# Attention outputs two units behind, and shared value rows written in by GpSimd

## The chip, the cores and the metric

The program runs on one core of a Trainium2 chip. The metric is device time in microseconds (us) of one execution; the median of three runs of the kernel before is 739.56 us (738.72 to 741.37).

## The reference, cut to what matters

Attention over 8 batches and 8 heads, with 512 local tokens and 32 global tokens of width 64, feeds a mixture of eight experts:

```python
k_all = concatenate([k_g, k_l]); v_all = concatenate([v_g, v_l])
out_g = softmax(scale * q_g @ k_all.T) @ v_all              # a global token sees everything
s_ll = where(abs(i - j) <= 32, scale * q_l @ k_l.T, -1e9)   # a local token sees a band
out_l = softmax(concatenate([scale * q_l @ k_g.T, s_ll])) @ v_all   # ... and the 32 global rows
x = concatenate([out_g, out_l]).reshape(4608, 512)
# each token goes to one of 8 experts (capacity 576, greedy by gate value): relu(x @ w1[e]) @ w2[e]
```

All inputs are float32. The host only rearranges them.

## The kernel before

**Two stages.** The attention takes the first 260 us of the profiled execution; the routing of tokens and the experts take the rest. The change touches the attention alone.

**Units.** For each batch there are ten units: eight `Local` units (half of the 512 rows of one pair of heads) and two `Glob` units (the global rows of four heads). 80 units in all. A unit passes through six steps, each an engine's work:

- `a`: scores on PE (TensorE) into the PSUM tile `S` (L143 of a local unit, L210 of a global one);
- `e`: mask and maximum on DVE (VectorE), which writes `p` and `nm` (L149, L151; L216 to L218);
- `f`: the exponentials on ACT (ScalarE) (L157; L228 to L234);
- `c`: transposes of `p` on PE into PSUM tile `T` (L162, L242), then a copy out of PSUM to `pt` or `pgt` on ACT (L269) or DVE (L271), three of five on ACT;
- `d`: the outputs on PE, `pt` times the value tile `vw`, into PSUM tile `O` (L174, L252), and their scaling by the row sum on DVE (`ls`, `xs`: L177, L178, L182). A global unit also stores its result to DRAM from SP (SyncE), four DMAs (L261).

**The order.** Each engine works through its own list in program order. The main loop, over `i`, puts into the lists: loads, `a` and `e` of unit i+2, `d` of unit i-1, `c` of unit i, `f` of unit i+2, and then the extra work of that step (the store of a finished batch `xd<-xs`, L186, and transposes and products for the gate, L277 to L292). So PE runs, in each step, the scores of a unit two ahead, the outputs of the unit one behind, and the transposes of the present one.

**The loads.** SP loads, for each of 32 pairs of heads, the queries `q` (272 KB), the keys `qk` (432 KB) and the value tile `vw` (1040 KB). It does so in step with the work: before each load a tiny DMA (`pace<-nm`, L123) waits for the maximum of the latest unit. GpSimd (POOL) spreads each `q` over a zero-padded tile `qz` in two copies (L87). Value tiles have six buffers.

**The value tile.** A local unit's 32 rows see a window of 128 key rows: three blocks of 32 local rows and the block of 32 global rows. `vw` holds, for each of 16 windows and two heads, these 128 rows on 128 partitions, 65 wide (64 values and a one, whose product is the row sum). So each tile holds the same 32 global rows 16 times for each head, all loaded from DRAM. In windows with odd number they lie on partitions 64 to 95, in those with even number on 32 to 63.

Of the kernel before, what the change touches and what calls it, by code (L numbers as in the profile page):

```python
# [8 lines left out]
F32 = mybir.dt.float32  # L9
# [9 lines left out]
B, H, SL, SG, D = 8, 8, 512, 32, 64  # L19
# [6 lines left out]
NB = SL // 128  # L26
NW = SL // 32
NZ = 6
NP = H // 2
# [6 lines left out]
def ap_of(t, offset, dims):  # L36
    return bass.AP(tensor=t.tensor, offset=t.offset + offset, ap=dims)
# [28 lines left out]
def attention(ctx, tc, A, consts, xd, pace, ident, L, nbatch, rt=None):  # L66
    nc = tc.nc
    ac = ctx.enter_context(tc.tile_pool(name="ac", bufs=1))
    ld = ctx.enter_context(tc.tile_pool(name="ld", bufs=3))
    wk = ctx.enter_context(tc.tile_pool(name="wk", bufs=3))  # L70
    ps = ctx.enter_context(tc.tile_pool(name="ps", bufs=2, space=PSUM))

    G = [(b, g) for b in range(nbatch) for g in range(2)]
    qk, vw, xs = {}, {}, {}

    def load_qk(b, p):
        t = ld.tile([128, KW], F32, name="qk", bufs=5)
# [10 lines left out]
        return spread  # L88

    def load_v(b, p):  # L90
        t = ld.tile([128, 2, NW, D + 1], F32, name="vw", bufs=6)
        nc.sync.dma_start(t.rearrange("p h w d -> p (h w d)"), A["vw"][b, p])
        vw[b, p] = t

    qz = [ac.tile([128, QW // 32, 2, 32], F32, name=f"qz{i}") for i in range(NZ)]
# [1 line left out]
    mask = ac.tile([128, 2 * NB, 128], F32, name="mask")  # L97
    wg = ac.tile([128, 4, 32], F32, name="wg")
# [27 lines left out]
    class Local:  # L126
# [32 lines left out]
        def c(s):  # L159
            t = ps.tile([128, NB, 128], F32, name="T", bufs=3)  # L160
            for c in range(NB):
                nc.tensor.transpose(t[:, c, :], s.p[:, c, :], ident)  # L162
            s.pt = wk.tile([128, NB, 128], F32, name="pt", bufs=3)
            evac(s.pt, t, bool(s.u) if s.b == nbatch - 1 and s.q == NP - 1 else None)

        def d(s):
            b, q, u = s.b, s.q, s.u
            o = ps.tile([128, 2, 2, D + 1], F32, name="O", bufs=2)
            for h in range(2):
                for k in range(2):  # L170
                    for r in range(4):
                        jj = 4 * k + r
                        lo = 64 * (jj % 2) + 32 * h
                        nc.tensor.matmul(o[32 * r:32 * r + 32, k, h, :], s.pt[:, jj // 2, lo:lo + 32],  # L174
                                         vw[b, q][:, h, 8 * u + jj, :], start=True, stop=True)
            ls = wk.tile([128, 2, 2], F32, name="ls", bufs=4)
            nc.vector.tensor_scalar(ls, o[:, :, :, D], 1e-9, None, op0=ALU.add)  # L177
            nc.vector.reciprocal(ls, ls)  # L178
            if q + u == 0:
                xs[b] = wk.tile([128, NB, DM], F32, name="xs", bufs=2)  # L180
            dst = xs[b][:, 2 * u:2 * u + 2, 128 * q:128 * q + 128].rearrange("p k (h d) -> p k h d", h=2)
            nc.vector.tensor_tensor(dst, o[:, :, :, 0:D], ls[:, :, :, None].to_broadcast([128, 2, 2, D]),  # L182
                                    op=ALU.mult)

    def store(b):
        nc.sync.dma_start(ap_of(xd, (b * S + SG) * DM, [[DM, 128], [128 * DM, NB], [1, DM]]), xs[b])  # L186

    class Glob:
# [22 lines left out]

        def e(s):
            b, g = s.b, s.g
            m = wk.tile([128, 8], F32, name="gm", bufs=2)
            s.m = m
            nc.vector.tensor_reduce(m[:, 0:1], s.sa, axis=AX.X, op=ALU.max)  # L216
            nc.vector.tensor_reduce(m[:, 1:2], s.sb, axis=AX.X, op=ALU.max)
            nc.vector.tensor_scalar(m[:, 2:3], m[:, 0:1], m[:, 1:2], -SCALE, op0=ALU.max, op1=ALU.mult)  # L218
# [16 lines left out]
                                 bias=m[:, 2:3], scale=SCALE, accum_out=m[:, 5:6])  # L235

        def c(s):
            s.pt = wk.tile([128, 6, 128], F32, name="pgt", bufs=2)
            for lo, n in ((0, 4), (4, 2)):
                t = ps.tile([128, NB, 128], F32, name="T", bufs=3)  # L240
                for k in range(n):
                    nc.tensor.transpose(t[:, k, :], s.p[:, lo + k, :], ident)  # L242
                evac(s.pt[:, lo:lo + n], t[:, :n])

        def d(s):
            b, g = s.b, s.g
            m = s.m
            o = ps.tile([128, D], F32, name="O", bufs=2)
            for k in range(6):
                for r in range(4):  # L250
                    h = 4 * g + r
                    nc.tensor.matmul(o[32 * r:32 * r + 32, :], s.pt[:, k, 32 * r:32 * r + 32],  # L252
                                     vw[b, h // 2][:, h % 2, 3 * k + 1 if k < 5 else 14, 0:D],
                                     start=(k == 0), stop=(k == 5))
            nc.vector.tensor_reduce(m[:, 6:7], m[:, 3:6], axis=AX.X, op=ALU.add)
            nc.vector.tensor_scalar(m[:, 6:7], m[:, 6:7], 1e-9, None, op0=ALU.add)
            nc.vector.reciprocal(m[:, 6:7], m[:, 6:7])
            xg = wk.tile([128, D], F32, name="xg", bufs=2)
            nc.vector.tensor_scalar(xg, o, m[:, 6:7], None, op0=ALU.mult)
            for r in range(4):  # L260
                nc.sync.dma_start(ap_of(xd, b * S * DM + (4 * g + r) * D, [[DM, SG], [1, D]]),  # L261
                                  xg[32 * r:32 * r + 32, :])
# [3 lines left out]
    def evac(dst, src, act=None):  # L266
        nev[0] += 1
        if nev[0] % 5 < 3 if act is None else act:
            nc.scalar.activation(dst, src, AF.Copy)  # L269
        else:  # L270
            nc.vector.tensor_copy(dst, src)  # L271
# [92 lines left out]
    units = []  # L364
# [8 lines left out]
    extra, wide = {}, {}  # L373
    GS = (0, 2, 4, 6, 8, 9)
    for b in range(nbatch):
        last = b == nbatch - 1
        s0 = 10 * (b + 1) + 1
        gl = gate_units(b, lambda b=b: gsrc[b // 4], 32 + b // 4, 1) if b % 4 == 3 else []
        lo = last_gate(b) if last else gate_units(b, lambda b=b: xs[b], 4 * b, NB)
        extra.setdefault(s0 + (-1 if last else 1), []).append(lambda b=b: store(b))  # L380
        if last:
            extra.setdefault(s0 - 5, []).append(lambda b=b: load_gx(b // 4))
            for k in range(3):
                extra.setdefault(s0 - (6, 4, 1)[k], []).append(lo[k])
        else:
            for k, f in enumerate(lo):
                (wide if k == 4 else extra).setdefault(s0 + (k if b == nbatch - 2 else GS[k]), []).append(f)
            if gl:
                extra.setdefault(s0 + 2, []).append(lambda b=b: load_gx(b // 4))
                for k, f in enumerate(gl):  # L390
                    (wide if k == 4 else extra).setdefault(s0 + 10 + k, []).append(f)
# [7 lines left out]
    nu = len(units)  # L399
    first = rt.setup(slice(0, 24), True) if rt else None  # L400
    LA = 2
    for i in range(-LA, nu + 3):
        if rt and i == 2:
            rt.load()
        if rt and i == 12:
            rt.prepare()
        if i + LA < nu:
            if i >= 0 and nl[1] < nl[0]:
                behind()
                load_v(*P[nl[1]])  # L410
                nl[1] += 1
            elif nl[0] < len(P) and nl[0] <= pairidx(units[i + LA]) + 3:
                if i >= 0:
                    behind()
                load_qk(*P[nl[0]])(nc.gpsimd)
                nl[0] += 1
            units[i + LA].a()
            units[i + LA].e()
            if i + LA == 0:
                spread1(nc.vector)  # L420
        if 1 <= i <= nu:
            units[i - 1].d()
        rest = [f() for f in wide.get(i, [])]
        if 0 <= i < nu:
            units[i].c()
        if i + LA < nu:
            units[i + LA].f()
        for f in rest + extra.get(i, []):
            f()
        if rt and i >= nu - 9:  # L430
            next(first, None)
# [733 lines left out]
def _layout(q_l, k_l, v_l, q_g, k_g, v_g, moe_w_gate, moe_w1, moe_w2):  # L1165
# [3 lines left out]
    qk = np.concatenate([qT, kT], axis=3).reshape(B, NP, 2 * D, QW + KW)  # L1169
# [1 line left out]
    st = [32 * ((3 * j + 1) // 2) for j in range(NW)]  # L1171
    vs = np.concatenate([vs, np.ones_like(vs[..., :1])], axis=3)
    vw = np.stack([vs[:, :, t:t + 128] for t in st], axis=3)
    vw = vw.reshape(B, NP, 2, 128, NW, D + 1).transpose(0, 1, 3, 2, 4, 5).reshape(B, NP, 128, 2 * NW * (D + 1))
    w1 = moe_w1.reshape(E, 4, 128, 2, FF // 2).transpose(3, 0, 2, 1, 4).reshape(2 * E * 128, 2 * FF)
    w2 = moe_w2.reshape(E, 2, 4, 128, DM).transpose(1, 0, 3, 2, 4).reshape(2 * E * 128, 4 * DM)
    wg = np.zeros((128, 4, 32), f)
    wg[:, :, :E] = moe_w_gate.reshape(4, 128, E).transpose(1, 0, 2)[:, :, ::-1]
    mask = np.full((128, 2 * NB, 128), 0.0, f)
    i = np.arange(32)  # L1180
    for j in range(NW):
        for w, bk in enumerate([j - 1, j, None, j + 1] if j % 2 else [j - 1, None, j, j + 1]):
            if bk is not None:
                t = 32 * bk + i
# [3 lines left out]
    p = np.arange(128)  # L1188
# [15 lines left out]
    k = np.arange(16)  # L1204
    for it in range(NIT):
# [7 lines left out]
    part = (p[:, None] // 32 == np.arange(4)[None])[:, None].repeat(5, 1)  # L1213
    part[:, 4] = np.arange(4) == 0
    cf[:, CPART:CPART + 20] = part.reshape(128, 20)
    a = dict(qk=qk, vw=vw, w1=w1, w2=w2, wg=wg.reshape(128, 128), mask=mask.reshape(128, 1024),
             ident=np.eye(128, dtype=f), cf=cf)
    return {n: np.ascontiguousarray(x) for n, x in a.items()}

# [14 lines left out]
```

## Time and profile before

| what | value |
|---|---|
| median of 3 runs | 739.56 us |
| the profiled execution: time, span | 736.8 us, 735.0 us |
| mean granted clock of TensorE | 0.966 |
| busy, share of the span: PE / DVE / ACT / POOL | 91% / 70% / 42% / 22% |
| moved by DMA | 120.61 MB, mean 164 GB/s |
| attention (about) | 0 to 262 us of the span |

The span runs from the first to the last instruction; 1.8 us of the profiled execution lie outside it. PE is the engine of the matmuls, PEld that of its weight loads. Idle time is put down to what ended it; "issue" is idle time of an engine that waited for nothing that the profile shows. The profile lists the DMA of the program's own instructions under a queue of its own, "instruction".

### The profile page before, as it was taken

The page shows a single profiled execution, that of the slowest core. Times are in us where ns is not written, and L with a number is a line of the kernel's source. Part 1 is how long each engine was busy: PE and PEld are TensorE (multiplying, and loading weights), DVE is VectorE, ACT ScalarE, POOL GpSimd, SP SyncE. Part 2 cuts the span into 40 slices and gives each one's busy share as a digit, 9 for nine tenths or more (in the row PEclk, how much of TensorE's full clock was granted, in tenths as well). Part 3 has the DMA queues.
Part 4 walks back from the last instruction along what each step waited for, and adds up shares of the span by engine and source line. Part 5 has one row for each costly group of instructions (what it writes and reads, how often), then busy time and mean ns, then how long its engine had stood idle before and what let it go on. Part 6 is the DMA issues. An engine that isn't in the chain of part 4 may idle for free.

```text
span 735.0 us, 22820 instructions
## 1 busy us (share of the span) xinstructions
PE 666.7 (91%) x9334; PEld 556.7 (76%) x9334; DVE 513.3 (70%) x2073; ACT 308.0 (42%) x839; POOL 163.8 (22%) x202
## 2 busy tenths in 40 slices
PE   7788787989879843999999999999999999999996
PEld 6566666767667633887897897897897898998985
DVE  5677576777677867898898798797897773451510
ACT  4455455566555511342444333343343343441510
POOL 5212111221212002304214214223213223412011
PEclk9999999999999975999999999999999999999999
DMA  9988777697876012505414432432433424514001
GB/s 352 369 293 295 237 252 258 228 343 228 324 258 228 12 59 75 216 2 173 180 46 149 158 115 79 159 130 79 149 143 108 166 90 152 189 33 158 16 19 43
DMA packets 32412, 120.61 MB, mean 164 GB/s; under 512 B 6836, under 2 KB 7092, under 8 KB 24116
## 3 DMA queue, kind: packets, MB, share of 16 engines
q1 hardware_dynamic: 21668, 66.73, 25.4%
q0 software_dynamic: 10640, 52.44, 20.6%
q8 instruction: 73, 1.20, 0.6%
q14 instruction: 31, 0.25, 0.1%
HBM read 101.32 MB, written 17.83 MB: 162 GB/s over the span
## 4 chain that ended last, share of the span: by engine, by line
PE 81%; DVE 10%; issue 5%; ACT 2%; DMA 2%; POOLq 0%; SPq 0%; DVEq 0%; ACTq 0%
PE H L1076 26%; PE Y L1102 24%; PE S L143 7%; PE O L174 4%; PE T L162 4%; PE R L564 3%; PE Y L1092 2%; PE H L902 2%; PE S L210 2%; PE T L277 1%; DVE p L149 1%; PE T L242 1%; PE O L252 1%; DVE pt L271 1%; PE O L283 1%
## 5 line engine op out<-in xcount | busy, mean ns | idle before, releaser
L1076 PE MATMUL H<-xh,w1h 128*128 128x272 f32 (+2 forms) x512 | 149.4, 292 | 0.9 <-ACT xh L875 0.8
L1076 PE MATMUL H<-xh,w1l 128*128 128x272 f32 (+2 forms) x512 | 149.8, 293 | 0.3 <-DVE w1l L489 0.3
L1076 PE MATMUL H<-xl,w1h 128*128 128x272 f32 (+2 forms) x512 | 148.7, 291 | 0.2 <-DVE xl L489 0.2
L1102 PE MATMUL Y<-w2h,hh 128*128 128x512 f32 x256 | 104.2, 407 | 0.0
L1102 PE MATMUL Y<-w2h,hl 128*128 128x512 f32 x256 | 103.3, 404 | 0.0
L1102 PE MATMUL Y<-w2l,hh 128*128 128x512 f32 x256 | 103.3, 404 | 0.0
L1079 ACT ACTIVATE hh<-H 128x272 fp32r<-128x272 f32 (+2 forms) x128 | 50.8, 397 | 113.5 <-PE H L1076 108.8
L1076 PEld LDWEIGHTS H<-xh,w1h 128*128 128x128 f32 x512 | 96.8, 189 | 1.7 <-ACT xh L875 1.1
L1076 PEld LDWEIGHTS H<-xl,w1h 128*128 128x128 f32 x512 | 96.4, 189 | 0.8 <-DVE xl L489 0.6
L1076 PEld LDWEIGHTS H<-xh,w1l 128*128 128x128 f32 x512 | 96.7, 189 | 0.4 <-DVE w1l L489 0.4
L157 ACT ACTIVATE p<-p,nm 128x128 f32<-128x128 f32 x256 | 81.4, 391 | 31.0 <-DVE ls L177 14.8
L149 DVE CUSTOM_DVE_ANT_0 p<-S,mask 128x128 f32<-128x128 f32 x256 | 59.0, 287 | 38.6 <-PE S L143 28.1
L143 PE MATMUL S<-qk,qz 128*32 128x128 f32 x2048 | 73.1, 279 | 11.9 <-issue 9.4
L87 POOL COPY qz<-q 64x544 f32<-64x544 f32 x60 | 38.2, 636 | 176.3 <-DMA q<-in_qk_dram 146.2
L143 PEld LDWEIGHTS S<-qk,qz 128*32 128x32 f32 x2048 | 53.5, 111 | 25.1 <-issue 21.6
L489 DVE SCALAR_TENSOR_TENSOR hl<-H,hh 128x272 fp32r<-128x272 f32 (+2 forms) x128 | 55.1, 435 | 20.5 <-ACT h L1081 14.0
L489 DVE TENSOR_TENSOR w2l<-w2r,w2h 128x512 fp32r<-128x512 f32 x64 | 41.9, 686 | 30.5 <-ACT w2h L875 30.0
L862 POOL DMA_INDIRECT xg<-xd,idx x40 | 39.6, 990 | 102.3 <-DVE idx L489 41.7
L174 PE MATMUL O<-vw,pt 128*32 128x65 f32 x2048 | 46.1, 227 | 14.2 <-issue 7.4
L1038 ACT ACTIVATE y<-Y 128x512 f32<-128x512 f32 x32 | 19.1, 598 | 94.7 <-PE Y L1102 80.8
L1102 PEld LDWEIGHTS Y<-w2h,hh 128*128 128x128 f32 x256 | 48.3, 189 | 10.3 <-issue 1.6
L1102 PEld LDWEIGHTS Y<-w2h,hl 128*128 128x128 f32 x256 | 48.3, 189 | 9.2
(183 smaller groups left out, 1163.6 us busy)
## 6 DMA issues: line engine op xcount, KB each, us to landing
vw<-in_vw_dram SPq DMA_DIRECT2D x32, 1040.0 KB
qk<-in_qk_dram SPq DMA_DIRECT2D x32, 432.0 KB
q<-in_qk_dram SPq DMA_DIRECT2D x32, 272.0 KB
xd<-xs SPq DMA_DIRECT2D x8, 1024.0 KB
xd<-xg SPq DMA_DIRECT2D x64, 8.0 KB
pace<-nm SPq DMA_DIRECT2D x58, 0.0 KB
xg<-xd,idx POOLq DMA_INDIRECT x40, 3.4
mask<-in_mask_dram SPq DMA_DIRECT2D x1, 512.0 KB
```

The lines of the kernel that those rows point to most:

```text
L87: eng.tensor_copy(z[r, :, h, :], q[r].rearrange("p (j i) -> p j i", i=32))
L143: nc.tensor.matmul(st[lo:lo + 32, c, :], z[:, j, h], kw[:, k0:k0 + 128], start=True, stop=True)
L149: nc.vector.tensor_tensor_reduce(s.p[:, c, :], st[:, c, :], mask[:, 4 * s.u + c, :], 1.0, -BIG, ALU.add, ALU.max, nm[:, c:c + 1])
L157: nc.scalar.activation(s.p[:, c, :], s.p[:, c, :], AF.Exp, bias=nm[:, c:c + 1], scale=SCALE)
L162: nc.tensor.transpose(t[:, c, :], s.p[:, c, :], ident)
L174: nc.tensor.matmul(o[32 * r:32 * r + 32, k, h, :], s.pt[:, jj // 2, lo:lo + 32], vw[b, q][:, h, 8 * u + jj, :], start=True, stop=True)
L489: return op(*args, **kw)
L564: s.nc.tensor.matmul(out, *args, **kw)
L862: nc.gpsimd.indirect_dma_start(out=dst, out_offset=None, in_=src, element_offset=off, in_offset=bass.IndirectOffsetOnAxis(ap=idx, axis=0))
L1076: nc.tensor.matmul(p, w[d][:, fs], x[:, d, q], start=(k == 0), stop=(k == 11))
L1079: nc.scalar.activation(hh[:, f, q], p, AF.Relu)
L1102: nc.tensor.matmul(p, h[:, f, q], w[f], start=(f + k == 0), stop=(f + k == 9))
```

## The change

**Outputs.** `d` of unit i-2 stands where `d` of unit i-1 stood; `pt` gets four buffers in place of three, `pgt` and `gm` three in place of two, and in the last batch the store and the last gate step come one step later.

**Value tiles.** The host lays the tile out by parity of the window. A load becomes four DMAs, of partitions 0 to 63 and 96 to 127 for odd windows and of 64 to 127 and 0 to 31 for even ones: 96 of 128 rows. Once per batch SP loads the global rows of all eight heads (`vg`, 64 partitions of 2080 B, which is the 32 rows twice), and for each pair GpSimd writes them into the tile in two copies, each to 32 partitions, 1040 elements in a partition, from 130 elements that are repeated eight times.

```diff
     def load_v(b, p):
-        t = ld.tile([128, 2, NW, D + 1], F32, name="vw", bufs=6)
-        nc.sync.dma_start(t.rearrange("p h w d -> p (h w d)"), A["vw"][b, p])
+        if p == 0:
+            g = ld.tile([128, NP, 2, D + 1], F32, name="vg", bufs=2)
+            nc.sync.dma_start(g[32:96].rearrange("p a h d -> p (a h d)"), A["vg"][b])
+            vg[b] = g
+        t = ld.tile([128, 2, 2, NW // 2, D + 1], F32, name="vw", bufs=6)
+        for par, lo, hi in ((1, 0, 64), (0, 64, 128), (0, 0, 32), (1, 96, 128)):
+            nc.sync.dma_start(t[lo:hi, par].rearrange("p h w d -> p (h w d)"), A["vw"][b, p, lo:hi, par])
+        for par in range(2):
+            q = slice(32 + 32 * par, 64 + 32 * par)
+            nc.gpsimd.tensor_copy(t[q, par], vg[b][q, p, :, None, :].to_broadcast([32, 2, NW // 2, D + 1]))
         vw[b, p] = t
...
-            s.pt = wk.tile([128, NB, 128], F32, name="pt", bufs=3)
+            s.pt = wk.tile([128, NB, 128], F32, name="pt", bufs=4)
...
-                                         vw[b, q][:, h, 8 * u + jj, :], start=True, stop=True)
+                                         vw[b, q][:, jj % 2, h, 4 * u + jj // 2, :], start=True, stop=True)
...
-            m = wk.tile([128, 8], F32, name="gm", bufs=2)
+            m = wk.tile([128, 8], F32, name="gm", bufs=3)
...
-            s.pt = wk.tile([128, 6, 128], F32, name="pgt", bufs=2)
+            s.pt = wk.tile([128, 6, 128], F32, name="pgt", bufs=3)
...
-        extra.setdefault(s0 + (-1 if last else 1), []).append(lambda b=b: store(b))
+        extra.setdefault(s0 + (0 if last else 1), []).append(lambda b=b: store(b))
...
-                extra.setdefault(s0 - (6, 4, 1)[k], []).append(lo[k])
+                extra.setdefault(s0 - (6, 4, 0)[k], []).append(lo[k])
...
-        if 1 <= i <= nu:
-            units[i - 1].d()
+        if 2 <= i <= nu + 1:
+            units[i - 2].d()
```

## Rows read from the trace of the kernel before

**Rows 1.** The windows view, five stretches: us, then each engine's busy time.

```profile
10.00:60.00 50.00, 41.11 (x1074) 31.11 (x1072) 36.39 (x209) 26.64 (x85) 11.70 (x20) 0.93 0.92 346
60.00:150.00 90.00, 76.55 (x2011) 58.53 (x2010) 60.69 (x328) 49.75 (x156) 14.01 (x22) 0.96 0.73 254
150.00:225.00 75.00, 64.40 (x1712) 49.83 (x1707) 53.78 (x286) 42.96 (x136) 14.69 (x24) 0.98 0.81 287
225.00:240.00 15.00, 14.84 (x420) 11.03 (x408) 11.71 (x60) 9.73 (x31) 2.70 (x5) 1.00 0.54 185
240.00:262.00 22.00, 18.83 (x488) 15.02 (x482) 16.19 (x86) 11.36 (x31) 0.50 (x1) 1.00 0.07 21
```

In each row stand PE, PEld, DVE, ACT and POOL (instructions in brackets), the granted clock, the DMA share and GB/s.

**Rows 2.** The waits view of PE, 0 to 262: total us, times, longest.

```profile
PE S L143 <- issue: 9.4, 8, 2.4
PE O L174 <- issue: 7.4, 5, 2.1
PE O L252 <- issue: 6.2, 4, 2.5
PE O L174 <- DVE pt L271: 5.1, 9, 1.1
...
PE O L174 <- ACT pt L269: 1.1, 3, 0.7
...
PE O L252 <- DVE pgt L271: 1.0, 1, 1.0
PE S L210 <- issue: 1.0, 1, 1.0
```

**Rows 3.** The windows view of two stretches, each from one stall's end to the next's.

```profile
122.22:128.08 5.86, 3.99 (x128) 3.56 (x127) 2.86 (x22) 2.24 (x6) 1.27 (x2) 1.00 0.92 369
213.28:219.41 6.13, 3.98 (x128) 3.56 (x127) 3.33 (x22) 3.35 (x10) 1.27 (x2) 1.00 1.03 406
```

**Rows 4.** The DMA view, 60 to 240: a queue, then two issues by size.

```profile
q8 instruction: 33, 0.54, 1.2%
...
vw<-in_vw_dram SPq DMA_DIRECT2D x22, 1040.0 KB
...
xd<-xs SPq DMA_DIRECT2D x6, 1024.0 KB
```

**Rows 5.** The timeline of PE around the longest stall.

```profile
73.00 0.52 PE L252 MATMUL O<-vw,pgt 128*32 128x64 f32 x24
76.02 0.55 PE L252 MATMUL O<-vw,pgt 128*32 128x64 f32 x24 [2.50 <-issue]
```

**Rows 6.** The DMA view, 69.9 to 73.4, just ahead of that stall.

```profile
DMA packets 174, 1.10 MB, mean 316 GB/s; under 512 B 17, under 2 KB 17, under 8 KB 50
```

**Rows 7.** The DMA view, 73.5 to 74.6: the instruction queue.

```profile
q8 instruction: 1, 0.02, 5.4%
```

**Rows 8.** The windows view, first and last of five stretches at lower granted clock.

```profile
29.36:32.77 3.41, 3.41 (x55) 2.28 (x49) 2.46 (x13) 1.28 (x4) 1.27 (x2) 0.50 0.86 320
...
220.50:223.91 3.41, 3.41 (x52) 1.93 (x52) 2.27 (x8) 0.30 (x1) 1.14 (x2) 0.50 0.83 308
```

**Rows 9.** The DMA view, 251.8 to 252.6: one 64 KB load to 32 partitions.

```profile
DMA packets 31, 0.07 MB, mean 82 GB/s; under 512 B 15, under 2 KB 15, under 8 KB 31
```

**Rows 10.** The view by line of POOL, 0 to 262: busy us, mean ns.

```profile
L87 POOL COPY qz<-q 64x544 f32<-64x544 f32 x60 | 38.2, 636 | 176.3 <-DMA q<-in_qk_dram 146.2 <-PE T L162 21.2 <-PE O L252 4.2
```

**Rows 11.** The view by source line, L151: duration ns min/median/max.

```profile
L151 DVE TENSOR_SCALAR nm<-nm x64: 169/170/639, 8.8 to 254.1; 128x4 f32<-128x4 f32 x64
```

**Rows 12.** The view by line of DVE, 0 to 262: busy us, mean ns, idle before.

```profile
L151 DVE TENSOR_SCALAR nm<-nm 128x4 f32<-128x4 f32 x64 | 13.1, 205 | 2.2
```

**Rows 13.** The timeline at 102 us: start us, us, engine, line.

```profile
102.27 0.64 POOL L87 COPY qz<-q 64x544 f32<-64x544 f32 x1 [5.40 <-PE T L162]
102.31 0.62 DVE L151 TENSOR_SCALAR nm<-nm 128x4 f32<-128x4 f32 x1
```

**Rows 14.** The view by source line, SP's value loads: duration ns min/median/max.

```profile
L92 SPq DMA_DIRECT2D vw<-in_vw_dram x32: 327/344/1140, 3.6 to 227.6; - x32
```

**Rows 15.** The waits view of SP, 0 to 245: total us, times, longest.

```profile
SPq L92 <- DMA mask<-in_mask_dram: 1.8, 1, 1.8
```

More of the change, by code (lines that the diff above doesn't have):

```diff
@@ L73, in attention @@
     G = [(b, g) for b in range(nbatch) for g in range(2)]
-    qk, vw, xs = {}, {}, {}
+    qk, vw, vg, xs = {}, {}, {}, {}
     def load_qk(b, p):
@@ L251, in d @@
                     h = 4 * g + r
+                    j = 3 * k + 1 if k < 5 else 14
                     nc.tensor.matmul(o[32 * r:32 * r + 32, :], s.pt[:, k, 32 * r:32 * r + 32],
-                                     vw[b, h // 2][:, h % 2, 3 * k + 1 if k < 5 else 14, 0:D],
+                                     vw[b, h // 2][:, j % 2, h % 2, j // 2, 0:D],
                                      start=(k == 0), stop=(k == 5))
@@ L1173, in _layout @@
     vw = np.stack([vs[:, :, t:t + 128] for t in st], axis=3)
-    vw = vw.reshape(B, NP, 2, 128, NW, D + 1).transpose(0, 1, 3, 2, 4, 5).reshape(B, NP, 128, 2 * NW * (D + 1))
+    vw = vw.reshape(B, NP, 2, 128, NW // 2, 2, D + 1).transpose(0, 1, 3, 5, 2, 4, 6).reshape(B, NP, 128, 2, NW * (D + 1))
+    vg = np.concatenate([v_g, np.ones_like(v_g[..., :1])], axis=3).transpose(0, 2, 1, 3).reshape(B, SG, H * (D + 1))
+    vg = np.concatenate([vg, vg], axis=1)
     w1 = moe_w1.reshape(E, 4, 128, 2, FF // 2).transpose(3, 0, 2, 1, 4).reshape(2 * E * 128, 2 * FF)
@@ L1215, in _layout @@
     cf[:, CPART:CPART + 20] = part.reshape(128, 20)
-    a = dict(qk=qk, vw=vw, w1=w1, w2=w2, wg=wg.reshape(128, 128), mask=mask.reshape(128, 1024),
+    a = dict(qk=qk, vw=vw, vg=vg, w1=w1, w2=w2, wg=wg.reshape(128, 128), mask=mask.reshape(128, 1024),
              ident=np.eye(128, dtype=f), cf=cf)
```

## The prediction

> **What bounds the kernel now.** I read the windows view first, to see which engine fills the attention. Where PE is undisturbed it is the bound: from 225 to 240 it is busy 14.84 of 15.00 us, while DVE is busy 11.71 and ACT 9.73 [rows 1]. From 10 to 225 it is busy only 182.1 of 215 us, so some 33 us are holes, and the question is what makes them.
>
> The waits of PE answer it [rows 2]. Idle time that ended with a copied `pt` or `pgt` is 5.1 + 1.1 + 1.0 = 7.2 us; this is what outputs two units behind can remove. Idle time called "issue" is far more: six rows from 9.4 down to 1.0 us (four are shown; the others are 2.1 and 1.8), 27.9 us in 21 stalls.
>
> What is "issue"? Between the ends of two neighbouring stalls PE and PEld run 128 + 127 instructions [rows 3]. From 60 to 240 the queue "instruction" moves 33 packets, 0.54 MB, 16 KB each [rows 4], while PE and PEld run 8268 instructions [rows 1]: 250 for each packet. So a packet is PE's next block of some 250 instructions, and a stall is a block that comes late. Why late? The longest stall begins at 73.5 and ends at 76.02 [rows 5]. Its one instruction packet starts only after 73.5 [rows 7]; in the 3.5 us before, 124 packets above 8 KB pass [rows 6], which are one value load (128 partitions of 8320 B) at 316 GB/s. The fetch stood behind the load. I looked at the sizes served ahead of each of the 21: in 16 stalls (20.0 us) a value load, alone or with queries and keys, in 5 (7.9 us) a 1024 KB store of `xs`. In the last 22 us, at a DMA share of 0.07, PE and PEld run 970 instructions [rows 1], some four blocks, and the one stall there follows a store.
>
> [...]
>
> **The change part by part**, against the profiled execution's own 736.8 us (735.0 span and 1.8 outside), which is 2.8 under the median of 739.6.
>
> *Outputs two behind.* `pt` is copied a whole step, some 3 us, before it is used, and `a` of another unit lies between. So the 7.2 us can go. Where such a wait stands shortly ahead of a stall, PE only reaches the late block sooner; and at the end the last outputs still wait for their own copy, with one unit's outputs between. I take 4; bounds 0 and 7.2. The three row-sum instructions and `xs` move with `d` on DVE and are used later by store and gate steps, which move along. Also moved are four DMAs on SP per global unit: stores that are read again tens of us later, except in the last batch, where 6 steps lie between. Value buffers are free one step later; loads run three pairs ahead, some 20 us, which hides it. If that cover were gone, a pair would be late by one step, 3 us.
>
> *Smaller value loads.* 260 of 1040 KB fall away per pair, 130 KB come per batch: 7.5 MB less, of some 66. Bandwidth alone buys little, as PE waits for data only in the first 10 us. What counts is the fetch. The load that it stands behind takes 1040 KB / 316 GB/s = 3.4 us [rows 6] and becomes four pieces. If a fetch waits for all that is ahead, it waits a quarter less, 0.85 us; taking 0.85 us (or all, where it is shorter) off each of the 16 stalls gives 11.7. If it waits only for the piece that an engine has in hand, the largest piece is a quarter of the old bytes and nearly all 20.0 go. The other bound: a piece reaches 32 or 64 partitions, and the nearest row for that, 64 KB to 32 partitions, shows 82 GB/s with its start and end in it [rows 9]; at that rate a load of 780 KB takes 9.7 us and a stall becomes longer. The value loads' own row is nearer (same queue, rows of kilobytes, several transfers in flight), so I take 13 off; bounds 20 off and 26 on (below).
>
> [...] No row here shows 64 partitions.
>
> *The clock.* With long stalls fewer, I take three of the five slow stretches as gone: 3 x 1.7 = 5; bounds 0 and 8.5.
>
> *GpSimd's copies.* 64 copies of 1040 elements to a partition. The nearest row, 544 elements in 636 ns [rows 10], gives 0.64 us (if only a start counted) to 1.22 us each; I take 1.2, as width counts, 77 us. GpSimd has room: in the 252 us from 10 to 262 it is busy 44 [rows 1], its queue mostly waits for `q` with 20 us in hand, and behind the copies stand only later spreads. If that cover went, each pair would be late by 2.4 us. But a copy holds up DVE: the instruction of L151 takes 170 ns as a median and 205 as a mean [rows 11, 12], and 620 when it meets a copy [rows 13]. Today that is 64 x 35 ns = 2.2 us. Twice the copy time and twice the length of one make it about 8 more; bounds 0 and 64 x 1.2 = 77. DVE is busy 179 of 252 us; with 8 more in a shorter attention of 233 it is at 80%, near the 78% at which PE ran full. I take 3 lost.
>
> *SP.* Three more issues per pair and one per batch, 104 x 0.34 us = 35 us [rows 14], on a queue that mostly waits. The second value load waited for the mask, eight transfers earlier, to land [rows 15], so SP keeps eight in flight, and four pieces use that up sooner. In the first 15 us this can delay a load; I take 1 lost, bounds 0 and 4.
>
> *Sum:* -4 - 13 - 5 + 3 + 1 = -18: 718.8 on the profile's scale, **721.5** as a median.
>
> **The rivals.**
>
> *All of it goes.* Every fetch behind a value piece is on time: -7.2 - 20.0 - 8.5, with little lost, gives about -33: 706. For it: pieces of a quarter. Against: stores, queries and keys stay and can now stand where the value load stood.
>
> *The fetch gains nothing.* Something else is ahead of it each time, and only the outputs count: -4 + 1: 736.5. For it: queries and keys of 704 KB follow each value load. Against: in 240 to 262, with little moved, the holes are gone. [...]
>
> *Slower: pieces are slow, and a fetch waits for the whole load.* If a load takes t in place of 3.4 us, 16 stalls grow by t - 3.4 each, against 4 gained by the outputs: it decides from t = 3.7 us. At half the rate, 158 GB/s, t is 5.0: +26 - 4, 762; at t = 4.2, 748. For it: the row of 32 partitions [rows 9]. Against: the four pieces lie on different partitions and can be in flight together. [...]
>
> *Slower: DVE becomes the bound*, each L151 waiting a whole copy: DVE needs 179 + 77 = 256 us, at 95% busy 269 in place of 252: +17, 757. It decides from 57 us of waiting on. Against: the mean excess today is 35 ns, where a met copy costs 450.
>
> **How the numbers follow.** Likeliest, 712 to 732: 0.46. All of it: 0.20. Fetch gains nothing: 0.15, half of it within 0.3% of 739.6 (737.4 to 741.8), which is about what can be told from no change. Slow pieces: 0.15. DVE: 0.04. Faster 0.46 + 0.20 + 0.08 = 0.74, same 0.07, slower 0.19. The range 705 to 743 leaves out part of the first rival below and most of the slow cases above, together 2 in 10.
>
> **What would show it.** Right: "issue" on PE under 17 us up to the end of attention, what is left standing behind `xs` stores; waits for `pt` under 3 us; two or fewer stretches at 0.50 before 225; POOL copies of 1.1 to 1.25 us; the mean of L151 near 330 ns. Wrong: value pieces that take over 4 us a load, issue idle above 28 us, or PE waiting for `nm`-fed exponentials or for `vw`.

## The result and the profile after

The changed kernel takes 742.33 us (median of 20 runs, 738.74 to 746.26) where the kernel before takes 737.0 (20 runs beside them, 732.17 to 741.68): ratio 1.007, 95% interval 1.0047 to 1.0093. It is slower by 0.7%, where a faster kernel was forecast: 721.5 (705 to 743).

The windows view of after, with the stretches and columns of [rows 1]:

```profile
10.00:60.00 50.00, 35.10 (x906) 27.79 (x909) 32.94 (x178) 23.70 (x76) 26.27 (x31) 0.91 0.95 248
60.00:150.00 90.00, 79.03 (x2138) 62.01 (x2133) 66.65 (x356) 53.59 (x166) 40.00 (x49) 0.99 0.87 242
150.00:225.00 75.00, 65.30 (x1791) 51.55 (x1786) 52.89 (x285) 42.47 (x134) 35.43 (x44) 1.00 0.89 250
225.00:240.00 15.00, 8.75 (x169) 4.83 (x161) 6.26 (x34) 5.71 (x18) 7.16 (x10) 0.86 0.78 207
240.00:262.00 22.00, 20.87 (x558) 17.63 (x550) 17.34 (x99) 13.69 (x40) 1.64 (x4) 0.94 0.22 69
```

Look at the last two columns first. Before, the DMA moved 346, 254 and 287 GB/s in the first three stretches at shares of 0.92, 0.73 and 0.81 [rows 1]; after, it moves 248, 242 and 250 at 0.95, 0.87 and 0.89. It is busier and moves less: the same engine time carries fewer bytes. Then count PE's instructions: from 10 to 225 us it runs as many as before (906 + 2138 + 1791 = 4835 against 4797 in [rows 1]), and from 225 to 240, where before it ran full with 420, it runs 169. There the last keys come too late, as the waits of PE show (0 to 262: us, times, longest):

```profile
PE O L182 <- issue: 9.3, 11, 1.7
PE S L151 <- DMA qk<-in_qk_dram: 6.7, 3, 3.8
PE S L218 <- DMA qk<-in_qk_dram: 5.7, 1, 5.7
PE S L151 <- issue: 5.5, 7, 1.7
PE S L151 <- ACT pg L239: 5.2, 3, 4.2
...
PE O L182 <- DVE pt L280: 0.7, 2, 0.4
```

Against [rows 2]: waits for `pt` fell from 7.2 to 0.7 us, issue from 27.9 to 17.5 (9.3 + 5.5 and three small rows). In their place PE waits 12.4 us for keys (before, 2.2, all in the first 10 us). The timeline of PE shows the two longest of these waits:

```profile
42.11 1.93 PE L151 MATMUL S<-qk,qz 128*32 128x128 f32 x32 [3.83 <-DMA qk<-in_qk_dram]
...
237.89 1.07 PE L218 MATMUL S<-qk,qz 128*32 128x512 f32 x6 [5.69 <-DMA qk<-in_qk_dram]
```

The late DMA also reaches DVE, by a way that I had not thought of. Four of the waits of DVE (10 to 266), then the timeline of SP and DVE at 28 us:

```profile
DVE p L157 <- DMA pace<-nm: 10.1, 5, 3.9
...
DVE p L157 <- PE T L170: 5.3, 2, 3.8
DVE p L157 <- PE T L286: 4.2, 1, 4.2
...
DVE p L157 <- PE O L182: 2.2, 1, 2.2
```

```profile
27.91 0.29 SPq L131 DMA_DIRECT2D pace<-nm  x1
...
31.23 0.29 DVE L157 CUSTOM_DVE_ANT_0 p<-S,mask 128x128 f32<-128x128 f32 x1 [3.87 <-DMA pace<-nm]
```

The tiny pacing DMA reads `nm`. Until it has read, DVE may not write that buffer of `nm` again; issued at 27.91 among the other transfers, it releases DVE at 31.23. The kernel before has no row for `pace` at all. The other three rows name transposes and outputs of PE, which this instruction of DVE does not read. Each of these waits ends within 0.25 us of the landing of a `pace` DMA, by the trace's semaphores; counted with them, DVE waits some 22 us for `pace`.

GpSimd's copies and DVE's instruction beside them, by line (0 to 265: busy us, mean ns):

```profile
L100 POOL COPY vw<-vg 32x1040 f32<-32x1040 f32 x64 | 67.0, 1047 | 15.6 <-DMA vg<-in_vg_dram 9.0
```

```profile
L159 DVE TENSOR_SCALAR nm<-nm 128x4 f32<-128x4 f32 x64 | 15.9, 249 | 2.2
```

The windows view of the stretches at half clock, first and last of four; there were five of 3.41 us before [rows 8]. The sum is 17 us in both, but here PE is idle in 3.6 of it (2.1 in the last row).

```profile
10.50:13.90 3.40, 3.40 (x44) 2.67 (x48) 2.48 (x16) 1.55 (x5) 2.08 (x2) 0.50 1.05 278
...
235.80:242.60 6.80, 4.71 (x67) 3.53 (x68) 1.93 (x8) 0.32 (x1) 4.29 (x6) 0.50 0.68 184
```

The attention's last output ends at 265.0 us instead of 259.5: of the 6.9 us by which the profiled span is longer (741.9 against 735.0), 5.5 lie in the attention.

### The profile page after: what moved, and what is told of

Read it like the earlier page. It is cut to its first block, busy times and chain, and to the rows that moved or that the text cites. A ratio compares the mean times of both kernels' runs of the same rounds, so it can differ in the third digit from the quotient of the medians.

```text
span 741.9 us, 23097 instructions
## 1 busy us (share of the span) xinstructions
PE 665.9 (90%) x9334; PEld 559.6 (75%) x9334; DVE 514.5 (69%) x2073; ACT 307.8 (41%) x839; POOL 231.3 (31%) x266
## 4 chain that ended last, share of the span: by engine, by line
PE 74%; DMA 10%; DVE 9%; issue 3%; ACT 1%; SPq 1%; POOLq 0%; DVEq 0%; ACTq 0%
PE H L1085 25%; PE Y L1111 23%; PE S L151 6%; DMA vw<-in_vw_dram 4%; PE T L170 3%; PE O L182 3%; PE R L573 3%; DMA qk<-in_qk_dram 2%; PE Y L1101 2%; PE H L911 2%; PE S L218 2%; PE T L286 1%; PE O L261 1%; PE T L250 1%; DVE p L157 1%
## 5 line engine op out<-in xcount | busy, mean ns | idle before, releaser
L151 PE MATMUL S<-qk,qz 128*32 128x128 f32 x2048 | 75.1, 285 | 21.8 <-DMA qk<-in_qk_dram 6.7
L151 PEld LDWEIGHTS S<-qk,qz 128*32 128x32 f32 x2048 | 55.9, 113 | 35.0 <-issue 19.9
L100 POOL COPY vw<-vg 32x1040 f32<-32x1040 f32 x64 | 67.0, 1047 | 15.6 <-DMA vg<-in_vg_dram 9.0
L498 DVE TENSOR_TENSOR w2l<-w2r,w2h 128x512 fp32r<-128x512 f32 x64 | 41.9, 685 | 30.8 <-ACT w2h L884 30.4
L923 POOL DMA_INDIRECT out_dram<-y,idx x32 | 32.9, 1029 | 79.0 <-ACT y L1047 42.6
```

Source lines behind the costliest of these rows:

```text
L100: nc.gpsimd.tensor_copy(t[q, par], vg[b][q, p, :, None, :].to_broadcast([32, 2, NW // 2, D + 1]))
L151: nc.tensor.matmul(st[lo:lo + 32, c, :], z[:, j, h], kw[:, k0:k0 + 128], start=True, stop=True)
L498: return op(*args, **kw)
L923: nc.gpsimd.indirect_dma_start(out=out, out_offset=bass.IndirectOffsetOnAxis(ap=rt.rows(ph, t)[:n], axis=0), in_=y[:n], in_offset=None)
```

## The experiments

My theory after the result: pieces of 32 and 64 partitions are slow, and the late transfers show up as late keys and as `pace`. Rivals: the number of transfers, GpSimd's copies, the wait for `pace` by itself, and one queue that serves the halves one after the other. Ratios are to the kernel before on the same chip, with 95% intervals.

### The two halves of the change, each alone

**e1_outputs**: the output edits (order, added buffers, store and gate step), old value loads. **e2_loads**: the new loads and GpSimd's copies, outputs one unit behind. The diffs are the two parts of the diff above.

> Only the outputs two units behind, value loads as before. Theory (the loss comes from value pieces that reach 32 or 64 partitions and are slow): 2 to 5 us faster than the kernel before, waits of PE for pt and pgt from 7.2 us to under 1.5, issue idle within 4 us of 27.9. Rival (the later outputs themselves cost, through buffers that come free a step later): 3 us or more slower.

> Only the new value loads and GpSimd copies, outputs one behind. Theory: 7 to 11 us slower than before, with the pieces' packets of 4160 B at a median near 260 ns, DVE waiting over 5 us for pace and PE over 8 us for keys. Rival (the later outputs cost): within 2 us of before.

Measured: e1_outputs 717.56 us, ratio 0.9693 [0.9657, 0.9729]. e2_loads 747.75, ratio 1.0101 [1.0067, 1.0136]. The loads cost 1% by themselves; the later outputs win 3%, far more than my 4 us in the forecast and the 2 to 5 expected here. The windows view of e1_outputs:

```profile
10.00:60.00 50.00, 41.33 (x1112) 32.42 (x1116) 37.05 (x216) 28.60 (x91) 11.79 (x20) 0.97 0.95 361
60.00:150.00 90.00, 79.44 (x2233) 63.13 (x2229) 68.29 (x363) 54.59 (x171) 18.60 (x30) 1.00 0.87 296
150.00:225.00 75.00, 69.54 (x1931) 55.04 (x1926) 59.51 (x323) 48.25 (x154) 12.94 (x21) 1.00 0.76 263
```

In the first two stretches, at the DMA shares that after has, it moves 361 and 296 GB/s where after moves 248 and 242, and PE gets through 206, 95 and 140 more instructions in the three stretches. In e2_loads the waits of PE and of DVE (0 to 266 and 10 to 300) show the chain from `pace` on:

```profile
PE O L182 <- DVE pt L280: 16.7, 12, 4.6
```

```profile
DVE p L157 <- DMA pace<-nm: 22.8, 8, 5.4
```

DVE waits for `pace`, its copies of `pt` come late behind that, and PE, whose outputs stand only one unit behind, waits for them. For keys it waits 5.4 us, where I had expected over 8.

### Width or number of transfers

Both keep all 1040 KB, the old order and four transfers of 260 KB per load. **e3_quarters** cuts by columns, **e4_halves** by partitions as well:

```diff
+        f = t.rearrange("p h w d -> p (h w d)")
+        for k in range(4):                               # e3_quarters
+            c = slice(520 * k, 520 * k + 520)
+            nc.sync.dma_start(f[:, c], A["vw"][b, p][:, c])
...
+        for lo, c in ((0, 0), (64, 1040), (0, 1040), (64, 0)):   # e4_halves
+            nc.sync.dma_start(f[lo:lo + 64, c:c + 1040], A["vw"][b, p, lo:lo + 64, c:c + 1040])
```

> The kernel before with each value load of 1040 KB cut into four transfers by columns, each of 128 partitions and 2080 B a row. Theory (width of the pieces, not their number): not slower than before by more than 1 us, no wait of DVE for pace, packets of 2080 B near 85 ns; issue idle falls from 27.9 to under 20, so up to 8 us faster. Rival (number of transfers: four issues and eight in flight hold SP up): 4 us or more slower, DVE waits for pace over 5 us.

> The kernel before with each value load of 1040 KB cut into four transfers of the same size as in the quarters, but of 64 partitions and 4160 B a row, alternately the lower and the upper 64. Theory (width): 8 us or more slower than before, packets of 4160 B at a median over 230 ns, DMA share from 60 to 225 over 0.88, DVE waits for pace. Rival (number of transfers): the same time as the quarters within 2 us.

Measured: e3_quarters 722.66 us, ratio 0.9754 [0.972, 0.9788]; e4_halves 777.21, ratio 1.0496 [1.046, 1.0531]. Same bytes, same count, same queue, 55 us apart; and the quarters win 17 us on before, where at most 8 were expected. The windows view from 60 to 150, e3_quarters and then e4_halves:

```profile
60.00:150.00 90.00, 80.42 (x2208) 62.78 (x2200) 68.44 (x367) 54.58 (x171) 17.09 (x27) 1.00 0.88 299
```

```profile
60.00:150.00 90.00, 73.30 (x1814) 57.34 (x1814) 57.08 (x318) 45.00 (x137) 13.60 (x23) 0.89 0.92 240
```

And e4_halves' waits, of DVE (10 to 300) and of PE (0 to 302):

```profile
DVE p L151 <- DMA pace<-nm: 63.6, 20, 6.5
```

```profile
PE O L176 <- DVE pt L273: 33.9, 12, 7.5
```

It is the width. The pieces also differ in the bytes to a partition (2080 and 4160), so compare packets of one size, counted over the records of the loads' packets: 4160 B to a partition take 161 ns as a median where a transfer covers 128 partitions (e6_two below), 282 where it covers 64 (e4_halves), 262 in the changed kernel. The queries' packets (2176 B) take longer beside such pieces, too: 88 ns as a median before, 107 in after (means 97 and 128). The keys' (3456 B) keep their median of 135, and their mean rises from 139 to 166.

### Both: later outputs with full-width pieces

**e5_both** is e1_outputs with e3_quarters' loads, **e6_two** the same with two column pieces (`range(2)`, 1040 columns).

> Outputs two behind and value loads of the whole 1040 KB in four transfers of 128 partitions by columns. Theory (the fetch waits for what one transfer has put ahead of it; both edits take stalls and slow clock away): 26 to 32 us faster than before, issue idle under 12 us, waits for pt under 1 us, at most one stretch at 0.50 in the attention. Rival (the two edits remove the same stalls, nothing adds up): 20 to 24 us faster, as with the outputs alone.

> As above with two transfers of 128 partitions by columns per value load. Theory: between the outputs alone (22 us faster) and the four transfers; if a fetch waits for one transfer's packets, issue idle lies between theirs. Rival (stalls do not depend on the size of a transfer): the same issue idle as the outputs alone, about 21 us.

Measured: 718.11 us, ratio 0.9767 [0.972, 0.9814], and 720.92, ratio 0.9791 [0.9745, 0.9836]. The gains don't add: the pieces win 17 us on the old order and nothing on the new one. The issue idle does fall with the size of a transfer, from 21.2 us in e1_outputs to 19.5 with two pieces and 12.5 with four, but no time is won by it, and both profiles have three stretches at half clock where e1_outputs' has one.

### Fewer bytes at full width

**e7_wide**: e1_outputs; three of four column quarters are loaded at 128 partitions. GpSimd writes the fourth in four copies from a tile loaded once per batch: the kernel leaves out that quarter's own values, and does all other work.

```diff
+        for k in range(3):
+            c = slice(520 * k, 520 * k + 520)
+            nc.sync.dma_start(f[:, c], A["vw"][b, p][:, c])
+        for k in range(4):
+            nc.gpsimd.tensor_copy(f[:, 1560:], vg[b])
```

> Outputs two behind; three of four column transfers of 128 partitions are loaded (780 KB, as many bytes as in the change), and GpSimd writes the fourth quarter of the tile from a tile that is loaded once per batch (260 KB), in four copies of 520 elements. The fourth quarter of the values is not the reference's; all other work is done. Theory (only the width of the pieces costs): within 4 us of the kernel with both edits, so 24 to 34 us faster than before. Rival (GpSimd's copies hold up DVE, or the spreads of the queries behind them): 10 us or more behind it.

Measured: 712.14 us, ratio 0.967 [0.9626, 0.9713]. By line, GpSimd's copies:

```profile
L100 POOL COPY vw<-vg 128x520 f32<-128x520 f32 x128 | 79.5, 622 | 11.0 <-DMA vg<-in_vg_dram 1.5 <-PE O L182 0.7 <-DMA vw<-in_vw_dram 0.5
```

With nearly after's bytes and 80 us of GpSimd's copies it is 30 us faster than after and some 6 faster than e5_both. So neither the copies nor the smaller number of bytes makes after slow. Whether fewer bytes at full width win anything over the output edits alone is not shown: their ratios, 0.9693 (e1_outputs) and 0.967, have intervals that overlap. e7_wide prices the idea; it is no version of the kernel.

### GpSimd's copies alone

**e13_copies**: e1_outputs, and for each pair two copies of after's kind into a tile that nobody reads. **e15_outputs_third**: e1_outputs again, on the same chip.

```diff
+        g = ld.tile([128, 8, 128], F32, name="vg", bufs=2)
+        for par in range(2):
+            q = slice(32 + 32 * par, 64 + 32 * par)
+            nc.gpsimd.tensor_copy(g[q], ident[q, None, :].to_broadcast([32, 8, 128]))
```

> Later outputs alone, with the old loads, and for each pair of heads two GpSimd copies of 32 partitions by 1024 elements into a tile that nobody reads (64 copies, some 1.05 us each, 67 us in all). Width theory (narrow transfers cost the time, the copies do not): within 3 us of later outputs alone, ratio to before 0.965 to 0.975. Rival (GpSimd's copies hold DVE up): DVE's nm instruction rises above 249 ns as a mean and the kernel is 5 us or more above later outputs alone, ratio 0.977 or above.

> Later outputs alone once more, beside the run with the copies on the same chip. If its gain is steady: ratio 0.966 to 0.974, issue idle in the attention 18 to 24 us and at most two stretches at half clock. If the gain was the chip's or the day's: ratio above 0.98.

Measured: 717.21 us, ratio 0.9749 [0.9673, 0.9824], beside 715.98, ratio 0.9731 [0.9663, 0.9799]. The copies cost 1.2 us, less than the intervals, of 5 us and more either way, can tell. By line, e13_copies:

```profile
L155 DVE TENSOR_SCALAR nm<-nm 128x4 f32<-128x4 f32 x64 | 19.2, 300 | 2.2
...
L96 POOL COPY vg<-ident 32x1024 f32<-32x1024 f32 x64 | 66.1, 1033 | 3.7
```

DVE is held up (300 ns against 215 in e15_outputs_third), and it does not show in the time. The gain of the later outputs holds in this third set of runs, and its issue idle is 19.2 us.

### The wait for `pace`, and the two queues

**e8_nm8**: after with ten buffers of `nm` in place of four (`bufs=10`). **e14_two_queues**: after with the pieces that start at partition 64 or 96 issued by GpSimd:

```diff
-            nc.sync.dma_start(t[lo:hi, par]...
+            (nc.gpsimd if lo >= 64 else nc.sync).dma_start(t[lo:hi, par]...
```

> The changed kernel with ten buffers of nm in place of four, so that DVE does not wait until pace has read an old one. Theory (the late SP queue reaches PE mostly through late keys and queries): waits of DVE for pace from 10 us to 0, and 1 to 6 us faster than the changed kernel. Rival (pace is the way in which the loss arises): 15 us or more faster than the changed kernel, near the outputs alone.

> The changed kernel, with the two pieces of each load that start at partition 64 or 96 issued by GpSimd, so that pieces of the lower and of the upper half lie in two queues and can be in flight together. If one queue that serves the halves one after the other is what makes narrow pieces slow: the DMA rate from 60 to 150 rises from 242 towards 290 GB/s and the ratio falls to 0.97 to 0.98. If narrow pieces are slow whatever stands beside them: rate under 255 GB/s and ratio 1.00 to 1.02; GpSimd's waits for buffers may add a few us, since the spreads of the queries stand behind them.

Measured: e8_nm8 741.91 us, ratio 1.0063 [1.0029, 1.0098]; e14_two_queues 741.77, ratio 1.0092 [1.0058, 1.0125]. Neither moves the time. In e8_nm8 DVE's row for `pace` is gone, and so are those that name transposes. PE waits longer for keys and queries instead (0 to 262), and DVE has a new row (10 to 266):

```profile
PE S L151 <- DMA qk<-in_qk_dram: 16.1, 7, 5.7
PE S L218 <- POOL qz L87: 4.7, 1, 4.7
...
PE S L218 <- DMA qk<-in_qk_dram: 3.5, 1, 3.5
```

```profile
DVE p L157 <- issue: 13.9, 5, 7.2
```

The three longest waits of that new row (7.2, 4.6 and 1.6 us) end 0.12 us after PE's semaphore, as other waits for scores do: DVE now waits for scores that are late themselves. So `pace` only carried the delay. In e14_two_queues the windows view from 60 to 150 shows the DMA full and no faster:

```profile
60.00:150.00 90.00, 76.70 (x2013) 60.24 (x2013) 67.87 (x351) 51.99 (x162) 52.60 (x75) 0.96 0.97 250
```

Narrow pieces are slow here with pieces of the other half in a queue beside them, too: 286 ns for a 4160 B packet. The loss takes another way, though. PE waits only 3.6 us for keys, and issue idle is 30.4 us.

### Why the later outputs win so much

**e9_buffers**: before with the added buffers alone. **e10_order**: also the outputs still one unit behind, but after the transposes of the present unit (`units[i - 1].d()` moved below `units[i].c()`), which gives the copy of `pt` more time. **e11_before_again** and **e12_outputs_again**: one more profile each of before and of e1_outputs.

> Only the added buffers of pt, pgt and gm; the order of the kernel before. Theory (the place of the outputs in PE's order gives the gain): within 2 us of before. Rival (the buffers do): 15 us or more faster.

> The outputs stay one unit behind, but stand after the transposes of the present unit instead of ahead of them, so that 1.2 us of other PE work in place of 0.6 lies between a copy and its use. Theory (the gain of the later outputs comes from the waits for pt, and from the slow stretches and stalls that go with them): waits for pt under 2 us, and 12 to 22 us faster than before. Rival (a whole unit of slack is needed): waits for pt above 4 us, at most 8 us faster.

> The kernel before, profiled once more, to see how much of its stalls and slow stretches is the same from one execution to the next. Theory: issue idle 24 to 32 us, waits for pt 6 to 9 us, four to six stretches at 0.50 ahead of 260. Rival (they are chance): under 20 us of issue idle, or at most two such stretches.

> The kernel with the outputs alone two behind, profiled once more. Theory: issue idle 18 to 24 us, no wait for pt, at most two stretches at 0.50 in the attention. Rival (the fall of the stalls and slow stretches was chance): issue idle above 26 us or four stretches or more.

Measured: e9_buffers 737.79 us, ratio 1.0027 [0.999, 1.0065]; e10_order 734.06, ratio 0.999 [0.9937, 1.0042]; e11_before_again 737.31 and e12_outputs_again 715.94, one run each. I split the end of the last output into idle time of PE (holes over 150 ns), half of the time at half clock, and the rest (us, from PE's records):

```
                    end     holes (issue, pt)   at half clock   rest
before             259.5    38.9 (27.9, 7.3)       17.1        212.1
e11_before_again   259.6    41.4 (29.9, 6.6)       13.7        211.3
e1_outputs         239.0    28.8 (21.2, 0)          3.4        208.5
e12_outputs_again  237.9    27.8 (22.5, 0)          3.4        208.5
e10_order          258.9    31.4 (26.3, 0.8)       17.1        218.9
after              265.0    45.5 (17.5, 0.7)       17.1        211.0
```

e10_order takes the waits for `pt` away and wins nothing: issue, slow stretches stay, and PE's work itself stretches from 212 to 219. Of the three edits only the whole unit of room wins; why PE's work takes longer in e10_order is open. (In after, 3.6 us of the time at half clock are also holes, so its rest is nearer 212.5. Either way PE's own work is, within 1 us, as long with the new layout of the value tile as before.) Of the 20.5 us that e1_outputs ends earlier, 7 are the waits for `pt`, 6.7 issue, 6.8 the clock (four stretches fewer at 1.7), 3.6 the rest, and other small waits take some 4 back. That issue and slow stretches fall with the order is steady over three profiles (issue 21.2, 22.5 and 19.2 us, one slow stretch each); why, no run shows. With other loads or copies beside the same order (e5_both, e6_two, e13_copies) there are three such stretches.

## Why the prediction was wrong

**The step that failed is "Smaller value loads".** For pieces to 32 and 64 partitions I took the rate of the whole load, 316 GB/s [rows 6], as nearer than the 82 GB/s of the one transfer to 32 partitions [rows 9], and booked 13 us won, all of it on the fetch. The fetch did gain: issue fell by 10.4 us, and by 18.9 in e2_loads, though part of that may only be hidden behind other waits. What I had put at nothing was the data ("Bandwidth alone buys little, as PE waits for data only in the first 10 us"). With narrow pieces the data come late: PE waits 12.4 us for keys in place of 2.2, and DVE some 22 for `pace`. e3_quarters against e4_halves shows that width decides, at equal count and bytes: 722.7 against 777.2. My argument that the four pieces "can be in flight together" failed as well: two queues did not help (e14_two_queues).

In the changed kernel the new loads, on top of an order that alone wins 3%, cost 25 to 28 us (1.007 less 0.969 to 0.973, of 737). On the old order they cost 7 to 8 (e2_loads). Why so different? The changed kernel, e2_loads, e8_nm8 and e14_two_queues all take between 741 and 748 us, whatever their order or waits, at 239 to 250 GB/s from 60 to 150. What fits all four is that the DMA sets the pace of the attention there, and that an order that lets PE go faster can't use it; no run shows this by itself. The sign that I had named, over 4 us for a load, does not tell the cases apart: from its first packet to the end of its last a load takes 4.9 us in the changed kernel, 4.2 before and 5.1 in e3_quarters (medians).

That 742.3 still lies inside the stated range is luck: the range was drawn around a faster kernel and leaves out most of the slow cases.

**The slower rival had the cause and not the way.** "Pieces are slow" came true. But it expected longer stalls of the instruction fetch, and issue fell: 27.9 to 17.5 us, 9.0 in e2_loads. (In e14_two_queues, where it is 30.4, the fetch may carry a part.) In the changed kernel the loss came as late keys and through `pace`, which I had counted as free. It gave 748 to 762, with stalls that didn't grow and only 4 for the later outputs.

What width costs a packet is seen in the records: 282 and 262 ns for 4160 B (e4_halves, the changed kernel) against 161 (e6_two), 1.6 to 1.75 times as long; and e14_two_queues found no help in a second queue, at 286 ns. The forecast had no row of a load to 64 partitions, and I gave slow pieces 0.15.

**Outputs two behind** was right in kind and mis-sized: the waits for `pt` went (7.2 to 0.7 us; 0 in e1_outputs), as forecast, but the step is worth 20 to 22 us by itself, not 4. It also takes some of what I had booked on the loads: issue and slow stretches. It fits that e3_quarters' 17 us and e1_outputs' 22 don't add.

**The clock**: 5 us won were forecast, and little came of it, since as much of the attention was granted half clock as before. The four stretches begin inside PE's four longest waits or at their end (10.5, 41.2, 58.3 and 235.8 us, waits of 2.2, 3.8, 4.2 and 5.7). In e1_outputs four of five stretches went. The 1.7 us a stretch in the forecast (8.5 for all five), and half of the time at half clock in the table above, are my estimate, half of 3.41 us at a granted 0.50 [rows 8]; that a stretch costs this much no run shows. What the trace of before shows: each of its five stretches begins 0.1 to 1.1 us after the end of a stall of 1.7 to 2.5 us, and a matmul of the 128x512 scores took 1062 ns as a mean in the last two (128.34 to 131.75, 220.50 to 223.91), 605 between the third and the fourth (80.55 to 128.34), at a granted 1.00.

**GpSimd's copies**: 1047 ns where I took 1.2 us; the mean of the held-up instruction 249 ns, not near 330; the cost 1.2 us (e13_copies), which the intervals tell neither from the 3 forecast nor from nothing. DVE did not become the bound: it is busy 66.65 of 90 us from 60 to 150. **SP**: one lost; not measured apart, since its new waits (19.5 us for keys and 12.5 for value pieces to land) are the slow transfers themselves.

Open: why the later outputs shorten the fetch's stalls and keep the clock up; whether a value tile laid out so that the smaller loads cover all 128 partitions would reach e7_wide's time, which wasn't tried, and whether that is below e1_outputs' at all. The better version here is the output edits alone, e1_outputs, at 0.969 to 0.973 of before.

## What to carry to other kernels

Before cutting bytes from a load, look at how many partitions each remaining piece covers: a quarter fewer bytes in pieces of 32 and 64 partitions made a slower load than all the bytes in one transfer over 128 (4.9 against 4.2 us, first packet to last). Read DMA share and GB/s together, stage by stage: here a higher share at a lower rate (0.87 and 242 GB/s from 60 to 150, where before had 0.73 and 254) came with the slower transfers, whichever wait then carried the delay. Measure the parts of a change apart: here one won 3% and the other hid it.

## What the hardware showed that I had not expected

A DMA of a few bytes can hold a compute engine: DVE waited up to 3.9 us at a time, 10.1 in all by the rows that name it, for a pacing DMA to read a tile that DVE was to write again (63.6 us in e4_halves). One load of 1040 KB cut into four of 128 partitions, nothing else changed, wins 2.5% on the old order: issue on PE falls from 27.9 to 15.4 us and no slow stretch is left in the attention. On the new order it wins nothing. And slow pieces slow their neighbours: the queries' packets take 107 ns in place of 88 as a median, while e1_outputs, at the same DMA share but with full-width loads, keeps them at 88.
